# Attention, leaky MLP and bilinear MLP on one core: the second sweep's blocks kept raw, and most accumulating transfers made into adds

## The chip, the core and the metric

One core of one Trainium2 chip runs the whole program. The metric is the device time of one execution, in microseconds. Engines are PE (TensorE), DVE (VectorE), ACT (ScalarE), POOL (GpSimd) and SP, which issues the plain transfers; POOL's queue issues the accumulating ones.

## What is computed

With 4 batches, 8 heads, 576 positions, 64 per head and 32 memory slots:

```
a = softmax(phi, over positions)
k_m, v_m = a^T k, a^T v                      # 32 x 64 for each batch and head
attn = softmax(q k_m^T / 8) v_m              # -> x: 2304 tokens x 512
h = x @ moe_w_in                             # 512 -> 2048
y = max(0.01 h, h) @ moe_w_out               # 2048 -> 512   (first MLP)
out = ((y @ w_a) * (y @ w_b)) @ w_out2       # 512 -> 1536 -> 512   (second MLP)
```

All of it is float32.

## The kernel before

Each matrix product is made as three matmuls of fp32r halves: an operand is split into a rounded copy ("hi", a CAST on ACT or DVE) and the rest ("lo", a subtraction on DVE). Most large products use a seven-product scheme for 2x2 blocks, so sums and differences of blocks (`S1` to `S4` of the weights, `T1` to `T4` of the data) are made on DVE and split too.

**First MLP.** Four chunks `c` of 512 of the 2048 columns, four batches. `v_m` is folded into `w_in` (`vw`, L682), `h` is made from the attention weights (L724, L733), the leaky ReLU gives `bt` (ACT, L700). `y_part` makes the seven products (`ys_x`, `ys_y`, `ys_z`, L873); their results are copied or joined into tiles `ok` and summed into the accumulators `acc` (`acc_of`, one for each batch and half of the columns, 128x1024). From chunk 1 on `y_out` (L892 on) adds a finished `ok` to its `acc` either on DVE or by an accumulating transfer from POOL's queue (L909), as the order table says.

**Second MLP.** Two sweeps `s` (two batches each) over 12 chunks `c` of 128 of the 1536 columns. `ab_unit` makes the seven products `abx`, `aby`, `abz` (L1081) from `yb`, the split blocks of the first MLP's output, and `wo`, the split weights; `left_unit` does the last 64 positions; `p_sums` makes the blocks `pb` of the elementwise product; `o_part` makes the second seven products (`os_x`, `os_y`, `os_z`, L1294) with `w2` (weight sums, `w2_sums`, L1206 on) and `wout2`, and sums into `oacc`, again by DVE or by an accumulating transfer (L1326); `o_unit` (L1159, products `o` L1184) makes what the scheme leaves; `store` writes out.

**What is kept in HBM.** Split weights of the first sweep are stored (`k_wo`, `k_wout`) and loaded back in the second (`w_back`, L1057). `y_blocks` (L942 to L980) makes the blocks of both sweeps as the first MLP ends: for the first sweep seven pairs that stay in SBUF, for the second seven pairs that are stored (14 stores `k_yb`, L965) and loaded back by `y_back` (L982 to L986) as the second sweep begins. `w2_sums` makes the weight sums once and stores the pairs (L1237); `w2_back` (L1197 to L1204) loads them in the second sweep.

**What sets the order.** Every instruction's place in the program is written by hand in the table `ORDER` (one number for each operation, with a suffix `a` for ACT, `v` for DVE, `g` for an accumulating transfer where there is a choice), and every tile's buffer in `PLACES` (37 + 9 buffers of SBUF, `s` and `g`, 6 small ones, 8 PSUM banks `b`). `Program.run` emits in that order; each engine and each queue works in order, and waits arise from data and from buffers that are used again.

Of the kernel before, what the change touches and what calls it, by code (L numbers as in the profile page):

```python
# [8 lines left out]
F32 = mybir.dt.float32  # L9
# [18 lines left out]
NB2 = 512  # L28
# [43 lines left out]
def c_dve(n):  # L72
    return 0.16 + n * 1.03e-3
# [13 lines left out]
9 15 14 17 21 40 12 22 11 8 23 62 43 41 16 7 24 2 44 65 18 46 25 26a 45 67 20 48a 82 84v 13 47 81 1 50a 42 28a 19 6 238 51 52 10 66 53 38 54a 3 29 60 55  # L87
59a 58a 83a 30 31 69 244 56a 57v 70 257 32a 33 250 239 242 71a 34a 35a 72a 39 240 5 4 61 241 91 37a 245 68 80 247 93 36a 92 27 243 79 248 94 258 0 95 246
249 96 252 97 264 261 259 98 99 278 265a 113 63 260 49 64 102 104 262 266a 251 312 263 253 85 254 103 255 313 86a 280 267 105 106 256 87 107 310 269v 270
268v 316 89a 279 117 88a 118 281 108 314 119 317 282 121 109 311 73 272 134 90 136a 78 165 110 74v 327 122 286 294 271 274 273 124v 120 275 315 75 76a 77a  # L90
329 324 283 143 328 321 115 145 144 146 123a 325 472 114 330 116 318 147 322 331a 333a 319 332 133 334 335 148 132 287 135a 295 168 149 338a 336a 170 297
296 288 337 150 348 131 298 154 473 169 339 344 289 151 156 320 155 157 290 184 158 130 159 186a 125 326 152a 160 172 161 153 162 126a 291 299 292v 174a
111a 137 475 476 349a 342 138a 323 478 346 142 300a 185 139 140a 171 127 129a 352 474 276v 277 128a 187a 302 100a 301 484 194 163a 164 195 141a 479 166 196
101 480 359 303 197 198 347 167 183 477 353a 350 487 376 284a 173 175a 343 361 360 379a 351 285 377a 517 380 305 199 200 201 357 205 345a 365 378 518 481
362 181 520 354 182 206 366 207 193 367 340 364 358a 381 202 208 363 355 521 203a 204 501 482 341 356 384a 374a 385 209 372a 375 486 188 176 368a 370a 751
382a 388 373 386 177a 189a 369 210 178 179a 502 190 192a 371 394 519 180a 383 304 389 191a 211 227 212 483 387 390 306a 213 229 503 214a 293 216 396 1316
490 492 391a 395a 1340 397 228 230 215 218 411 522 418 491 504 217 219 220 509 1322 510 231 221 412 222 421a 485 223 400 505 401 224 494 506 405 406 402
407 512 488 403 232 493 233 419a 225a 404a 408 414a 392 393 226 733 398 409 413 234 420 410 422 735 308a 423 415 430 424a 399a 734 431 426a 428 235 432 112
# [12 lines left out]
731a 523a 900 788 732 877 1005 884 782 783 866 807 837a 878 1008 808 524 876g 1006 858 871 791 903a 1367 1369 1007 912 885 859 901a 872 862 838 768a 907
839a 873 1017 863 794 864 850 1011 846 847 852 795 904 851 861 879 769 902 913 886 1374a 1376a 944 1377 867 1014 881 776a 798a 882 868 916 883 1375 840
1012 797 880 921 1416 887a 947a 1390 777 796 799 1009 888 933 908 922a 930 931 889 934 905 917a 1013 1417 906 936 938 925 926 939 1420 1419 937 1418 890a
1389 1020 935 918 1421 800a 891 951 895 932g 920 892 893v 923 801 919 956 924 1023 898a 894 1010 952a 914 915 927 909 945a 820g 899 946 1019 929 957a 960
1018 928 961a 948 1015 967 965 966v 911 910 949 792a 793 896a 897 1392 958 1025 1016 950 1422a 1393 1423 968 959 1021 1022 1026 1424 981 1024 1027 953 940a
954 972 969g 955 942a 941 973 977 962 963 1429 1028 1395 986 982 1398 784v 987 974 976 1029 1081 975 1394 1030a 785 964 970 943 1082a 971 1400 989 983 979
1031 1032a 1033 985 1090 984 990a 1085 980 1401 1091 1076 1077a 991 1083 1058 1084 992 1100 978 1059 1086 1087 998 1399 1402 1089 1088 1095 993a 1074 1099
1101 988g 1060 1396 1397 999a 1408a 1092g 1078 1042 1079 994 1080 1409 1062 1075 1102 995 1061 1003a 996a 1063 1093 1094 1425 1107 997 1108a 1104 1096 1034
1103a 1120 1403 1001a 1050 1000 1004 1002 1125 1043 1045 1410a 1098 1126a 1121a 1127 1128 1129g 1097 1113 1116a 1036 1046 1137 1114a 1117 1404 1106 1115
1132 1052 1141 1035 1105 1405 1130 1407 1406 1037 1414a 1038 1411 1426 1133 1044 1131 1134 1146 1412a 1122 1047 1053 1051 1454 1138 1415 1123 1136 1172  # L120
1413 1124 1147 1179 1142 1436 1173a 1175a 1176 1428 1111a 1135 1054 1039 1427 1184 1040a 1174 1109a 1055 1438 1139 1140 1185 1156 1118 1119 1066 1439 1041
1143 1145 1157 1144 1153 1154 1110 1149 1150 1158 1151 1155 1159a 1188 1048a 1216 1180 1067 1070a 1069 1068 1049 1152 1199 1189a 1071 1164 1217a 1201 1219a
1112 1195 1193 1160 1196 1186 1197 1430 1431 1194a 1218 1187 1202 1198 1716 1437 1208 1200 1170a 1161 1433 1167 1162a 1210 1203 1204g 1177 1440 1441 1207
1163 1171 1165a 1209 1211 1457 1072a 1190 1191 1455 1223 1148g 1192 1456 1220 1073 1178 1166 1442 1448a 1228 1224a 1056a 1432 1449 1057 1434 1181 1458 1205
1229a 1206 1232 1435 1459 1168a 1183 1237 1182 1225 1233a 1239 1464 1064a 1443 1238a 1169 1227 1212a 1230 1253 1226 1554 1231 1221 1444 1234 1222 1214a
1255 1065 1213 1249 1257 1240 1258 1577 1256 1215 1462 1460a 1251 1236 1254 1259 1235 1261 1252 1260g 1244 1242 1461 1246 1277 1467 1250 1262a 1263 1243
1551 1247 1264 1283 1245 1279 1267 1265a 1281 1278a 1268a 1280a 1266 1288 1273a 1521 1270 1271a 1710 1290 1241g 1289a 1269 1284 1291a 1468a 1287 1272 1294
1601 1292 1282 1295a 1274 1520 1470 1719 1293a 1297 1248 1285g 1473 1286 1296 1450a 1298g 1305 1717 1445 1452a 1469 1451 1453 1476 1301 1711 1525 1580 1466
1306 1303 1304 1474a 1299 1477a 1275a 1475 1307g 1606 1302 1276 1526a 1484a 1528 1300 1471a 1481 1552 1314 1485 1516a 1556 1315 1517 1529a 1479a 1312 1446a
1308 1480 1532 1478 1578 1465 1310 1447 1579 1563 1522 1713 1557a 1502 1523 1482a 1507a 1519 1311 1559 1472 1509 1488a 1530 1531a 1558 1553 1492 1565 1581  # L130
# [146 lines left out]
def tile_mem_attention__leaky_mlp__bilinear_mlp(  # L277
# [664 lines left out]
    def y_blocks(s, due):  # L942
# [11 lines left out]
        def pair(name):  # L954
            g, t = at[name]
            hi, lo = ("yb", s, name, 0, 0), ("yb", s, name, 1, 0)
            for k in (hi, lo):
                tile_of(k, "slot", [2, NB2], F32R)
# [441 lines left out]
    for s in range(2):  # L1400
        if s:
            y_back(1)
# [67 lines left out]
```

## Time and profile before

| | us |
|---|---|
| median of 3 runs | 765.59 |
| lowest, highest | 765.35, 765.61 |
| profiled execution, own time | 768.98 |
| its span in the profile | 767.2 |
| PE busy | 750.8 |
| DVE busy | 642.2 |
| ACT busy | 495.8 |
| POOL busy | 29.4 |

The span runs from the first to the last instruction of the profiled execution. A busy share is the mean over stages that differ, so the windows of the section with the rows give it by stretch. An engine's idle piece is put down to what came last before it, by the semaphores that the profile shows.

### The profile page before, as it was taken

The numbers are of one execution on the slowest core, as the hardware profiler recorded it, in microseconds if no ns is written. First come the engines' busy times: TensorE is split into PE (matmuls) and PEld (weight loads), VectorE is DVE, ScalarE is ACT, GpSimd is POOL, SyncE is SP. The second block draws the span as 40 slices with busy tenths as digits, with TensorE's granted clock in tenths as the row PEclk, the third lists the DMA queues.
The fourth block names the chain that finished last, engine by engine and source line by source line (L and its number), as shares of the span: only waits on it lengthen the run. The fifth ranks groups of instructions, "written<-read, shape, count | busy, mean of one in ns | idle before, by whom it ended". The sixth has DMA issues, their size and how long they took to land.

```text
span 767.2 us, 12233 instructions
## 1 busy us (share of the span) xinstructions
PE 750.8 (98%) x4492; PEld 618.0 (81%) x4492; DVE 642.2 (84%) x1040; ACT 495.8 (65%) x975; POOL 29.4 (4%) x39
## 2 busy tenths in 40 slices
PE   8899999999999999989999999999999999999997
PEld 7656778887898878878888888888878888878886
DVE  2888988988799899989988899989999775766776
ACT  4889999778788788856566757686652423333430
POOL 0000000000001000010000000000000000010100
PEclk9999999999999999999999999999999999999999
DMA  8986502535545664578889787797999899797955
GB/s 318 343 328 234 193 1 97 193 97 160 147 133 147 142 194 136 151 226 240 289 303 324 290 256 261 265 303 276 320 378 317 293 310 359 251 248 262 314 114 166
DMA packets 66059, 179.84 MB, mean 234 GB/s; under 512 B 8016, under 2 KB 21584, under 8 KB 66000
## 3 DMA queue, kind: packets, MB, share of 16 engines
q1 hardware_dynamic: 61248, 161.76, 59.7%
q0 software_dynamic: 4752, 17.30, 12.1%
q8 instruction: 35, 0.57, 0.3%
q14 instruction: 24, 0.20, 0.1%
HBM read 109.84 MB, written 51.90 MB: 211 GB/s over the span
## 4 chain that ended last, share of the span: by engine, by line
PE 81%; DMA 6%; ACT 5%; issue 4%; DVE 3%; POOL 0%; SPq 0%; DVEq 0%; POOLq 0%; ACTq 0%
PE abx L1081 14%; PE h L733 12%; PE ys_x L873 9%; PE os_x L1294 7%; PE abz L1081 7%; PE ys_z L873 4%; PE os_z L1294 4%; PE aby L1081 4%; PE o L1184 3%; PE yl L817 2%; PE ys_y L873 2%; PE vw L682 2%; PE a L1126 2%; PE b L1126 2%; PE os_y L1294 2%
## 5 line engine op out<-in xcount | busy, mean ns | idle before, releaser
L1081 PE MATMUL abx<-yb_T,wo 128*128 128x512 f32 x432 | 109.0, 390 | 0.9 <-DMA wo<-k_wo_-1_1_3_2771 0.9
L1081 PEld LDWEIGHTS abx<-yb_T,wo 128*128 128x128 f32 x432 | 80.2, 188 | 17.5 <-issue 1.3
L311 ACT COPY ok<-os_x 128x512 f32<-128x512 f32 x66 | 38.3, 587 | 57.7 <-PE os_x L1294 49.6
L733 PE MATMUL h<-ahi,vwh 128*128 128x320 f32 (+1 forms) x240 | 72.3, 301 | 0.4 <-ACT bt L700 0.4
L733 PE MATMUL h<-alo,vwh 128*128 128x320 f32 (+1 forms) x240 | 71.1, 296 | 0.0
L733 PE MATMUL h<-ahi,vwl 128*128 128x320 f32 (+1 forms) x240 | 71.0, 296 | 0.0
L700 ACT ACTIVATE bt<-h 128x256 f32<-128x256 f32 x120 | 45.6, 389 | 23.1 <-PE h L733 19.7
L733 PEld LDWEIGHTS h<-ahi,vwh 128*128 128x128 f32 x240 | 45.4, 189 | 10.2 <-issue 2.6
L311 ACT COPY pf<-abx 128x512 f32<-128x512 f32 x48 | 27.9, 585 | 36.4 <-PE abx L1081 34.1
L733 PEld LDWEIGHTS h<-alo,vwh 128*128 128x128 f32 x240 | 45.4, 189 | 1.9
L733 PEld LDWEIGHTS h<-ahi,vwl 128*128 128x128 f32 x240 | 45.4, 189 | 0.0
L316 DVE TENSOR_TENSOR sl_T<-bt,sh_T 128x1024 fp32r<-128x1024 f32 x28 | 34.2, 1220 | 8.1 <-ACT sh_T L311 6.0
L1294 PE MATMUL os_x<-pb_T,w 128*128 128x512 f32 x132 | 36.3, 392 | 1.7 <-ACT ok L311 1.6
L1081 PE MATMUL abx<-yb_B,wo 128*128 128x512 f32 x144 | 36.7, 390 | 0.0
L1081 PE MATMUL aby<-yb_B,wo 128*128 128x512 f32 x144 | 36.7, 390 | 0.0
L1081 PE MATMUL abz<-yb_B,wo 128*128 128x512 f32 x144 | 36.6, 391 | 0.1
L1081 PE MATMUL abz<-yb_T,wo 128*128 128x512 f32 x144 | 36.3, 390 | 0.0
L316 DVE TENSOR_TENSOR bt<-bt,bt 128x1024 f32<-128x1024 f32 x28 | 33.8, 1218 | 0.7 <-ACT bt L700 0.4
L311 ACT CAST sh_T<-bt 128x1024 fp32r<-128x1024 f32 x27 | 28.5, 1055 | 6.7 <-DMA k_wout_-1_3932<-wout_-1_3888 3.8
L1081 PEld LDWEIGHTS abz<-yb_B,wo 128*128 128x128 f32 x144 | 26.8, 188 | 6.0 <-DVE u L316 0.5
L1081 PEld LDWEIGHTS abx<-yb_B,wo 128*128 128x128 f32 x144 | 26.8, 188 | 5.9 <-issue 0.4
L1081 PEld LDWEIGHTS abz<-yb_T,wo 128*128 128x128 f32 x144 | 26.9, 188 | 5.7
(318 smaller groups left out, 2011.3 us busy)
## 6 DMA issues: line engine op xcount, KB each, us to landing
k_wo<-wo SPq DMA_DIRECT2D x32, 512.0 KB, 6.5
wo<-k_wo SPq DMA_DIRECT2D x32, 512.0 KB, 5.6
raw_wout<-in_w_out_dram SPq DMA_DIRECT2D x24, 512.0 KB, 4.6
acc<-ok POOLq DMA_DIRECT2D x18, 512.0 KB, 5.1
kv<-in_kv_dram SPq DMA_DIRECT2D x16, 512.0 KB, 9.3
raw_win<-in_w_in_dram SPq DMA_DIRECT2D x16, 512.0 KB, 6.7
oacc<-ok POOLq DMA_DIRECT2D x15, 512.0 KB, 8.0
k_w<-w SPq DMA_DIRECT2D x10, 512.0 KB, 6.0
```

The costliest lines, as they stand in the source:

```text
L311: nc.scalar.copy(dst, src)
L316: nc.vector.tensor_tensor(dst, a, b, op=alu)
L682: nc.tensor.matmul(T[os[i]][k * M:(k + 1) * M, :], vm[half, k, b, :], w, start=True, stop=True)
L700: nc.scalar.activation(dst, src, AF.Prelu, alpha=0.01)
L733: nc.tensor.matmul(T[o], T[w[u]][:, k, fs], T[a[v]][:, k, cols], start=k == 0 and y == 0, stop=k == 1 and y == 2)
L817: nc.tensor.matmul(T[o], T[ws[j]][:, u, w_left(c, 2 * eh + j, i, x)], T[hl[v]][:, f, :], start=f == 0 and y == 0, stop=f == 3 and y == 2)
L873: nc.tensor.matmul(T[o], lhs(T, u, w_left(c, 0, kk, x)), T[hl[v]][:, kk, :], start=i in (1, 2, 5) and kk == 0 and y == 0, stop=kk == 1 and ...
L1081: nc.tensor.matmul(T[o], T[w][:, which, u, k * P:(k + 1) * P], T[ys[v]][:, k, :], start=first and k == 0 and x == 0, stop=k == 1 and x == ...
L1126: nc.tensor.matmul(T[o], T[w][:, k // 2, u, k % 2 * P:(k % 2 + 1) * P], T[ys[v]][:, k, :], start=(k == 0 and x == 0), stop=(k == 3 and x = ...
L1184: nc.tensor.matmul(T[o], T[w][:, u, es], right(T, x, v), start=(x == 0 and k == 0), stop=(x == 1 and k == 2))
L1294: nc.tensor.matmul(T[o], lhs(T, u), T[g][:, v, :], start=i in (1, 2, 5) and k == 0, stop=k == 2, skip_group_check=True)
```

## The change

1. The second sweep's four accumulators `acc(2,·)` and `acc(3,·)` are stored as they are when the first MLP ends (`y_keep`, 4 stores) and loaded raw as the second sweep begins (`y_back`, 4 loads into `acb`). The four differences and the seven splits are made there, the differences in place of the `acb` tiles.
2. `w2_back` and the stores of `w2` are gone; `w2_sums` runs in both sweeps, from `wf`, which is loaded again in the second (5 loads of 512 KB more).
3. Of 33 accumulating transfers 5 are left; the others are adds on DVE.
4. `ORDER` and `PLACES` are new throughout (3065 operations, 3060 before).

```diff
-    def y_blocks(s, due):
+    def y_blocks():
...
-            for k in (hi, lo):
-                if s == 0:
-                    tokens[k] = [k]
-                else:
-                    op("DMA", c_dma(524288), lambda T, k=k: nc.sync.dma_start(kept(k), T[k].bitcast(F32)), r=[k], w=[("kept", k)], tiles=[k], ahead=1e12)
...
+    def y_keep(due):
+        for l in range(2):
+            for j in range(2):
+                g = ("acc", 2 + l, j)
+                op("DMA", c_dma(524288), lambda T, g=g: nc.sync.dma_start(kept(g), T[g]), r=[(g, x) for x in range(2)], w=[("kept", g)], tiles=[g], ahead=1e12, due=due)
+
+    def y_back():
+        at = {}
+        for l, j in ((0, 0), (1, 0), (1, 1), (0, 1)):
+            k, g = ("acb", l, j), ("acc", 2 + l, j)
+            tile_of(k, "slot", [2, NB2])
+            op("DMA", c_dma(524288), lambda T, k=k, g=g: nc.sync.dma_start(T[k], kept(g)), r=[("kept", g)], w=[k], tiles=[k], ahead=40.0)
+            at[f"B{j + 1}{l + 1}"] = k
+        into = {"T1": "B11", "T2": "T1", "T3": "B12", "T4": "B21"}
+        for name, x, y in Y_SUMS:
+            if x:
+                g, a, b_ = at[into[name]], at[x], at[y]
+                op("DVE", c_dve(2 * NB2), lambda T, g=g, a=a, b_=b_: minus(T[g], T[a], T[b_]), r=[a, b_], w=[g], tiles=list(dict.fromkeys((g, a, b_))), ahead=25.0)
+                at[name] = g
+            y_pair(1, name, at[name], [at[name]])
...
-    def w2_back(q):
...
-            if s == 0 and by_seven(1, 2 * q):
-                op(
-                    "DMA", c_dma(524288), lambda T, k=k: nc.sync.dma_start(kept(k).rearrange("p a b -> p (a b)"), flat(T[k])),
...
-                    if s and by_seven(0, c):
-                        w2_back(c // 2)
-                    else:
-                        w2_sums(s, c // 2)
+                    w2_sums(s, c // 2)
```

`y_pair` is the old `pair` without its store: a copy that rounds and a subtraction.

Three places show the order. POOL's queue, all its accumulating transfers after the set-up, here the last ones of before (`acc` are the first MLP's accumulators, `oacc` the second's with the sweep as their first number):

```order
L1326 DMA oacc_0_1_0_4723<-ok2_0_5_6_6726 128x1024
L1326 DMA oacc_1_1_1_7127<-ok2_1_1_7_7244 128x1024
L1326 DMA oacc_1_1_0_7159<-ok2_1_1_6_7198 128x1024
L1326 DMA oacc_1_0_0_7006<-ok2_1_1_1_7191 128x1024
L1326 DMA oacc_1_0_0_7006<-ok2_1_2_1_7422 128x1024
L1326 DMA oacc_1_1_0_7159<-ok2_1_2_6_7469 128x1024
```

and all of the change:

```order
L909 DMA acc_1_0_1235<-ok_3_0_6_3762 128x1024
L1312 DMA oacc_0_0_0_4749<-ok2_0_2_1_5469 128x1024
L1312 DMA oacc_0_1_1_4693<-ok2_0_2_7_5512 128x1024
L1312 DMA oacc_0_1_0_4732<-ok2_0_2_6_5491 128x1024
L1312 DMA oacc_0_0_0_4749<-ok2_0_3_1_5887 128x1024
```

Of 33 rows 5 are left, one on `acc` and four on the first sweep's `oacc`; none is left in the second sweep.

SP's queue where the first sweep begins, before (`k_` is a place in HBM, left of the arrow for a store):

```order
L1057 DMA wo_0_0_1_4244<-k_wo_-1_0_1_1897 128x1024
L965 DMA k_yb_1_B22_1_0_4250<-yb_1_B22_1_0_4168 128x1024
L965 DMA k_yb_1_B21_0_0_4261<-yb_1_B21_0_0_4248 128x1024
L1057 DMA wo_0_1_3_4280<-k_wo_-1_1_3_2771 128x1024
L1033 DMA k_wo_-1_3_0_4324<-wo_-1_3_0_4186 128x1024
L965 DMA k_yb_1_B22_0_0_4337<-yb_1_B22_0_0_4158 128x1024
L965 DMA k_yb_1_B21_1_0_4350<-yb_1_B21_1_0_4287 128x1024
L965 DMA k_yb_1_B11_0_0_4352<-yb_1_B11_0_0_4263 128x1024
```

and with the change:

```order
L1057 DMA wo_0_0_3_4238<-k_wo_-1_0_3_1867 128x1024
L392 DMA raw_wb_7_0_4241<-in_w_b_dram 128x4x128
L1057 DMA wo_0_1_1_4263<-k_wo_-1_1_1_2302 128x1024
L970 DMA k_acc_2_1_4266<-acc_2_1_1690 128x1024
L970 DMA k_acc_3_0_4269<-acc_3_0_1684 128x1024
L392 DMA raw_wa_6_0_4280<-in_w_a_dram 128x4x128
L1057 DMA wo_0_2_1_4305<-k_wo_-1_2_1_3453 128x1024
```

The stores of split blocks are gone from between the loads of `wo`, and two of the four stores of accumulators stand there, each behind nothing but the accumulator itself.

DVE's queue shortly before the second sweep's first product, with the change (`acb` are the raw blocks, `yb_1` the second sweep's split ones, `ok2` the joins of the second MLP):

```order
L316 TENSOR_TENSOR ok2_0_4_6_6283<-os_0_4_0_z_6279,ok2_0_4_6_6283 128x512
L316 TENSOR_TENSOR yb_1_B21_1_6349<-acb_0_1_6313,yb_1_B21_0_6315 128x1024
L316 TENSOR_TENSOR pt_11_6166<-b_11_6222,pt_11_6166 128x256
L316 TENSOR_TENSOR acb_0_0_6007<-acb_1_1_6329,acb_0_0_6007 128x1024
L316 TENSOR_TENSOR acb_1_0_6054<-acb_1_1_6329,acb_1_0_6054 128x1024
L316 TENSOR_TENSOR oacc_0_1_0_4732<-oacc_0_1_0_4732,ok2_0_3_6_6025 128x1024
L316 TENSOR_TENSOR acb_0_1_6313<-acb_0_1_6313,acb_0_0_6007 128x1024
L316 TENSOR_TENSOR oacc_0_0_1_4639<-os_0_4_1_x_6331,oacc_0_0_1_4639 128x512
```

None of the `acb` and `yb_1` rows stood here before; the add on `oacc` is a row of the kind that takes the place of an accumulating transfer.

## Rows read from the trace of the kernel before

**Rows 1.** The page, part 1: busy us, share of the span, instructions.

```profile
PE   750.8 (98%) x4492; PEld 618.0 (81%) x4492; DVE 642.2 (84%) x1040; ACT 495.8 (65%) x975; POOL 29.4 (4%) x39
```

**Rows 2.** Window: us, PE, PEld, DVE, ACT, POOL busy, PEclk, DMA share, GB/s.

```profile
0.00:80.00 80.00, 73.92 (x795) 49.74 (x796) 56.82 (x116) 62.97 (x153) 0.69 (x6) 1.00 0.84 298
```

**Rows 3.** PE's timeline (start, us, what) at five stalls, then its waits.

```profile
339.18 0.50 PE L873 MATMUL ys_x<-sh_T,wsh 128*128 128x512 f32 x1 [1.96 <-ACT ok L311]
...
372.20 1.16 PE L1081 MATMUL abx<-yb_T,wo 128*128 128x512 f32 x4 [0.90 <-DMA wo<-k_wo_-1_1_3_2771]
...
422.85 1.42 PE L1184 MATMUL o<-plf,wout 128*128 128x256 f32 x9 [0.58 <-ACT oaccl L311]
...
511.45 0.98 PE L1184 MATMUL o<-plf,wout 128*128 128x256 f32 x6 [0.63 <-DVE oaccl L316]
...
690.43 0.98 PE L1294 MATMUL os_x<-pb_T,w 128*128 128x512 f32 x3 [1.56 <-ACT ok L311]
...
PE tz L506 <- ACT en L311: 1.8, 1, 1.8
PE h L724 <- DVE at L642: 0.7, 1, 0.7
```

**Rows 4.** Other engines' timeline, and the chain, around those stalls.

```profile
327.34 1.21 DVE L316 TENSOR_TENSOR bt<-bt,bt 128x1024 f32<-128x1024 f32 x1
327.72 1.75 POOL L909 DMA_DIRECT2D acc<-ok  x2 [17.12 <-DVE ok L316]
328.48 0.68 DVE L316 TENSOR_TENSOR wout_-1_3888<-cv_wout,wout_-1_3888 128x512 fp32r<-128x512 f32 x1
329.22 0.32 SPq L1033 DMA_DIRECT2D k_wout_-1_3932<-wout_-1_3888  x1
337.60 1.04 ACT L311 CAST sh_T<-bt 128x1024 fp32r<-128x1024 f32 x1 [3.79 <-DMA k_wout_-1_3932<-wout_-1_3888]
...
353.11 10.22 DMA acc<-ok
...
360.04 7.29 SPq L965 DMA_DIRECT2D k_yb_B<-yb_B  x2
363.35 0.62 ACT L311 CAST wo_-1_3_0_4186<-cv_wab 128x512 fp32r<-128x512 f32 x1 [5.16 <-DMA acc<-ok]
...
409.62 8.70 DMA raw_wa<-in_w_a_dram
...
507.51 0.62 ACT L311 CAST wout<-cv_wout 128x512 fp32r<-128x512 f32 x1 [2.74 <-DMA oacc<-ok]
...
678.33 10.37 DMA oacc<-ok
```

**Rows 5.** Accumulating transfers: issues by kind, KB each, median us to landing.

```profile
acc<-ok POOLq DMA_DIRECT2D x18, 512.0 KB, 5.1
oacc<-ok POOLq DMA_DIRECT2D x15, 512.0 KB, 8.0
```

**Rows 6.** DVE's groups by line and form: busy us, mean ns of one, idle before.

```profile
L316 DVE TENSOR_TENSOR oacc<-oacc,ok 128x1024 f32<-128x1024 f32 x12 | 14.6, 1216 | 0.0
L316 DVE TENSOR_TENSOR w<-w2s,w 128x512 fp32r<-128x512 f32 x12 | 8.2, 685 | 1.3 <-ACT w L311 1.3
L316 DVE TENSOR_TENSOR w2s<-wf 128x256 f32<-128x256 f32 x12 | 4.8, 416 | 1.7 <-DMA wf<-k_wf 1.7
L447 DVE TENSOR_REDUCE nmx<-phi 128x2 f32<-128x1152 f32 x3 | 4.0, 1345 | 1.6 <-DMA phi<-in_phiT_dram 1.6
```

**Rows 7.** Windows between marks that both orders have, columns as above.

```profile
520.20:597.70 77.50, 76.98 (x385) 64.23 (x384) 72.34 (x130) 42.25 (x78) 0.00 (x0) 1.00 0.88 320
597.70:683.30 85.60, 85.60 (x382) 70.96 (x382) 60.24 (x95) 30.17 (x55) 3.44 (x4) 1.00 0.88 292
683.30:767.20 83.90, 78.29 (x343) 62.90 (x341) 57.31 (x88) 26.62 (x46) 6.07 (x7) 1.00 0.74 219
```

**Rows 8.** A window of 20 us with DVE nearly full, same columns.

```profile
460.00:480.00 20.00, 20.00 (x115) 17.52 (x114) 19.67 (x40) 15.66 (x31) 0.00 (x0) 1.00 0.72 266
```

More of the change, by code (lines that the diff above doesn't have):

```diff
@@ L940, in kept @@
         return places[k]
-    def y_blocks(s, due):
-        acc = lambda l, j: ("acc", 2 * s + l, j)
-        made = lambda l, j: [((acc(l, j)), x) for x in range(2)]
-        yt = {n: ("yt", s, n) for n in ("T1", "T2", "T3", "T4")}
-        at = {f"B{j + 1}{l + 1}": (acc(l, j), made(l, j)) for j in range(2) for l in range(2)}
-        at.update({n: (k, [k]) for n, k in yt.items()})
-        def minus_of(name, x, y):
-            tile_of(yt[name], "slot", [2, NB2])
-            (a, ta), (b_, tb) = at[x], at[y]
-            op("DVE", c_dve(2 * NB2), lambda T: minus(T[yt[name]], T[a], T[b_]), r=[*ta, *tb], w=[yt[name]], tiles=[yt[name], a, b_], ahead=1e12, due=due)
-        def pair(name):
-            g, t = at[name]
-            hi, lo = ("yb", s, name, 0, 0), ("yb", s, name, 1, 0)
-            for k in (hi, lo):
-                tile_of(k, "slot", [2, NB2], F32R)
-            op(copy_by(2 * NB2), 0, lambda T, e: copy(e, T[hi], T[g]), r=t, w=[hi], tiles=[hi, g], ahead=1e12, due=due)
-            op("DVE", c_dve(2 * NB2), lambda T: minus(T[lo], T[g], T[hi].bitcast(F32)), r=[*t, hi], w=[lo], tiles=[hi, lo, g], ahead=1e12, due=due)
-            for k in (hi, lo):
-                if s == 0:
-                    tokens[k] = [k]
-                else:
-                    op("DMA", c_dma(524288), lambda T, k=k: nc.sync.dma_start(kept(k), T[k].bitcast(F32)), r=[k], w=[("kept", k)], tiles=[k], ahead=1e12)
-                    back = (*k[:4], 1)
-                    tile_of(back, "slot", [2, NB2], F32R)
-                    tokens[back] = [back]
-        pair("B11")
-        minus_of("T1", "B12", "B11")
-        pair("T1")
-        minus_of("T2", "B22", "T1")
-        pair("T2")
-        minus_of("T3", "B22", "B12")
-        pair("T3")
-        pair("B21")
-        minus_of("T4", "B21", "T2")
-        pair("T4")
-        pair("B22")
@@ L982, in y_back, with y_pair @@
-    def y_back(s):
-        for name in YB:
-            for i in range(2):
-                k, back = ("yb", s, name, i, 0), ("yb", s, name, i, 1)
-                op("DMA", c_dma(524288), lambda T, k=k, back=back: nc.sync.dma_start(T[back].bitcast(F32), kept(k)), r=[("kept", k)], w=[back], tiles=[back], ahead=25.0)
+    def y_pair(s, name, g, t, due=None):
+        k = [("yb", s, name, v) for v in range(2)]
+        for x in k:
+            tile_of(x, "slot", [2, NB2], F32R)
+            tokens[x] = [x]
+        ahead = 25.0 if s else 1e12
+        op(copy_by(2 * NB2), 0, lambda T, e: copy(e, T[k[0]], T[g]), r=t, w=[k[0]], tiles=[k[0], g], ahead=ahead, due=due)
+        op("DVE", c_dve(2 * NB2), lambda T: minus(T[k[1]], T[g], T[k[0]].bitcast(F32)), r=[*t, k[0]], w=[k[1]], tiles=[*k[::-1], g], ahead=ahead, due=due)
@@ new lines, in tile_mem_attention__leaky_mlp__bilinear_mlp @@
+    Y_SUMS = (("B11", None, None), ("T1", "B12", "B11"), ("T2", "B22", "T1"), ("T3", "B22", "B12"), ("B21", None, None), ("T4", "B21", "T2"), ("B22", None, None))
+    def y_blocks():
+        acc = lambda l, j: ("acc", l, j)
+        at = {f"B{j + 1}{l + 1}": (acc(l, j), [(acc(l, j), x) for x in range(2)]) for j in range(2) for l in range(2)}
+        for name, x, y in Y_SUMS:
+            if x:
+                g = ("yt", name)
+                tile_of(g, "slot", [2, NB2])
+                (a, ta), (b_, tb) = at[x], at[y]
+                op("DVE", c_dve(2 * NB2), lambda T, g=g, a=a, b_=b_: minus(T[g], T[a], T[b_]), r=[*ta, *tb], w=[g], tiles=[g, a, b_], ahead=1e12)
+                at[name] = (g, [g])
+            y_pair(0, name, *at[name])
@@ new lines, in y_keep @@
+    def y_keep(due):
[11 more added lines that the diff above has]
+        into = {"T1": "B11", "T2": "T1", "T3": "B12", "T4": "B21"}
+        for name, x, y in Y_SUMS:
+            if x:
+                g, a, b_ = at[into[name]], at[x], at[y]
+                op("DVE", c_dve(2 * NB2), lambda T, g=g, a=a, b_=b_: minus(T[g], T[a], T[b_]), r=[a, b_], w=[g], tiles=list(dict.fromkeys((g, a, b_))), ahead=25.0)
+                at[name] = g
+            y_pair(1, name, at[name], [at[name]])
@@ L1075, in product @@
             i, which = PLACE[left]
-            w, ys = ("wo", s, c, i), [("yb", s, right, v, s) for v in range(2)]
+            w, ys = ("wo", s, c, i), [("yb", s, right, v) for v in range(2)]
             def prod(T):
@@ L1195, in o_unit @@
             store(s, l, e, acc, i, (ka, cut[0]) if cut else ka, cut)
-    def w2_back(q):
-        for i in range(2):
-            k, there = ("w2", 1, q, i), ("w2", 0, q, i)
-            tile_of(k, "slot", [2, 2, 256], F32R)
-            op(
-                "DMA", c_dma(524288), lambda T, k=k, there=there: nc.sync.dma_start(flat(T[k]), kept(there).rearrange("p a b -> p (a b)")),
-                r=[("kept", there)], w=[k], tiles=[k], ahead=40.0,
-            )
     def w2_sums(s, q):
@@ L1234, in w2_sums @@
             )
-            if s == 0 and by_seven(1, 2 * q):
-                op(
-                    "DMA", c_dma(524288), lambda T, k=k: nc.sync.dma_start(kept(k).rearrange("p a b -> p (a b)"), flat(T[k])),
-                    r=[k], w=[("kept", k)], tiles=[k], ahead=1e12,
-                )
     def p_sums(s, q, odd):
@@ L1395, in tile_mem_attention__leaky_mlp__bilinear_mlp @@
     pr.due = None
-    y_blocks(0, None)
+    y_blocks()
     y_left_blocks()
-    y_blocks(1, (step + 1, 0))
+    y_keep((step + 1, 0))
     queue = []
@@ L1401, in tile_mem_attention__leaky_mlp__bilinear_mlp @@
         if s:
-            y_back(1)
+            y_back()
         for c in range(NC2):
```

257 lines of the change are left out of this document (128 added, 129 removed).

## The prediction

> **What bounds the kernel now.** I read the busy table first. TensorE (PE) is busy for 750.8 of 767.2 us with 4492 matmuls [rows 1]; the change leaves their number and shapes as they are, so only PE's 16.4 us of idle time can be won, and anything that adds idle time is lost at once. Next I read the windows: 6.1 us of the idle time lie in the first 80 us (80.00 less 73.92, [rows 2]) and 5.6 from 683.3 on (83.90 less 78.29, [rows 7]), the rest in small pieces; PE's granted clock reads 1.00 in each of these rows, which here is the 2.4 GHz level, so clock plays no part. PE's own timeline and list of waits [rows 3] name what came last before each idle piece, and most names are ACT or DVE. So I followed each back through the chain and the other engines' timelines [rows 4], and there five stalls turn out to be made by transfers:
> - At 339.18 PE waits 1.96 us for ACT. ACT itself stood 3.79 us until the store of `wout` had read its buffer. That store was issued at 329.22, just behind two accumulating transfers issued at 327.72, and had still not let go of its buffer 8 us later.
> - At 372.20 PE waits 0.90 us for a load of `wo`. SP (the queue of plain transfers) was held for 7.29 us from 360.04 on by two stores of `yb_B` ahead of it; those hung on ACT, which stood 5.16 us for an accumulating transfer that took 10.22 us.
> - At 422.85, 0.58 us: behind a load of `raw_wa` that took 8.70 us.
> - At 511.45, 0.63 us: ACT had stood 2.74 us for an accumulating transfer.
> - At 690.43, 1.56 us: ACT's `ok`, and before it ACT's `pb_B`, came behind an accumulating transfer of 10.37 us that ended at 688.70.
>
> Together 5.6 us. In three of the five an accumulating transfer of `ok` is the cause itself; in the others the queues are crowded. The list of transfers shows why those are bad to wait for: a median of 5.1 (`acc`) and 8.0 us (`oacc`) from issue to landing [rows 5].
>
> **The change, part by part.**
> *Transfers.* 10 stores and 10 loads of split blocks go (14 of each become 4), 10 stores and 10 loads of split weight sums become 5 loads, and 28 of 33 accumulating transfers go: 63 transfers of 0.524 MB, 33 MB. The four first-MLP blocks that are stored now are the accumulators themselves, so no split stands ahead of their stores, and the two stores that held SP at 360.04 don't exist. ACT's waits at 363, 507 and 689 have no accumulating transfer left to wait for: after the change only one `acc` and four `oacc` transfers remain, all before the second sweep. I take all five stalls as gone, −5.6 us; the bounds are −5.6 and 0 (each replaced by a wait of its own length).
>
> A page speaks against the cause. The Trainium skill, DMA: Bandwidth & Descriptors, section Anatomy of one DMA — SWDGE (gpsimd) path, has a transfer from this queue last about 2.0 us and its bytes at 436 GB/s, which for 524288 bytes would be an estimate of 3.2 us. This case's rows don't agree: their medians are 5.1 and 8.0 us, and 10.22 and 10.37 on the chain. By that rule nothing of the 5.6 us would come back, and the time would be that of rival 1.
>
> *DVE's added work.* 28 adds of 128x1024 at 1.216 us (17 on `acc`, 11 on `oacc`) are 34.0 us [rows 6]. The five sets of weight sums made again cost 5 × (4 × 0.416 + 2 × 0.685) = 15.2 us. The subtractions and splits of the `yb` blocks are as many as before, only later. DVE thus goes from 642 us [rows 1] to about 690 of 760. Where it lies decides. I went through DVE's rows in both orders between marks that both have (the first `pf<-abx` of a chunk) and summed them by the means of [rows 6] and their like. Up to 520.2 us the sums differ by 7.8 us in all (2.8 of small copies before 109.7, 6 in 109.7 to 347.7, 1 less after that, since 7 splits leave). DVE's free time there is 67.8 us: 767.2 less 642.2 for the whole span [rows 1], less 5.2, 25.4 and 26.6 in the three stretches behind 520.2 [rows 7]. So I count nothing. From 520.2 (chunk 8 of the first sweep) to 597.7 (first chunk of the second) it is 7.1 more: 4 subtractions and 6 splits arrive, older weight work leaves. From 597.7 to 683.3 it is 27.2 more: 19 rows of weight sums, 8 splits of them, 3 adds, and joins that were done later before. After 683.3 it is 11.6 more, in 26.6 us of free time.
> So the stretch 520.2 to 683.3 has to take 34.3 us. From that I subtract the overlap of neighbours: the rows at 327.34 and 328.48 start 1.14 us apart where the first lasts 1.21 [rows 4], 0.07 us for each of 50 added rows, 3.5 us. That leaves 30.8. The stretch has 5.16 + 25.36 = 30.5 us free on DVE [rows 7]. How far can gaps be filled? In the 20 us from 460 on DVE is busy 19.67 and PE all 20.00 [rows 8]; so a nearly full DVE doesn't stop PE by itself, but 1.65% stays open, 2.7 us of 163.1. DVE's cost is 0.3 + 2.7 = **+3.0 us**. The lower bound is 0 (work runs on past 683.3, where time is free). For the upper one, if only two thirds of the gaps can be filled, because DVE works in order and a gap is a wait for a product, it is 30.8 − 20.3 = +10.5. I take the low value since the row at a full DVE is the nearest one.
>
> *Prologue.* The phi reduction of batch 1 is put first on DVE, and between the score transposes and the first `at` DVE now does one clamp and one join of weights, not two each, some 1.1 us less. The first `h` waits 0.7 us for exactly this `at` [rows 3]. I take −1.0. At best the 1.8 us wait of `tz` goes with it (−2.5); at worst the reduction ahead of everything (1.345 us, [rows 6]) delays the first scores as a whole (+1.4).
>
> *The raw blocks' latency.* SP has the first two loads of `acb` among the stores of chunks 9 and 10, well ahead of the second sweep's first product. 0; at worst one more stall like that at 372, +0.9 [rows 3].
>
> *The tail.* PE's last products stand in the same order. Three `oacc` adds stand among DVE's last joins, one before, beside the last nine groups of `o` products. 0; at worst the two more, +2.4 [rows 6].
>
> Sum: −5.6 + 3.0 − 1.0 = −3.6 us. The profiled execution took 768.98 (span 767.2) and would take 765.4; it lies 3.4 above the median of the runs, 765.59, so against that median the forecast is **762.0 us**.
>
> **Rivals.**
> 1. *Accumulating transfers were not what held PE.* If a transfer that is short on its own only looked late because ACT or SP reached its consumer late, the 5.6 us stay in another form: −1.0 + 3.0 = +2.0, **767.6 us**. For it: two of five stalls name no accumulate. Against it: 10.22 and 10.37 us measured on the very chain. The rule of the Trainium skill quoted above would make this case.
> 2. *Waits only change places.* The adds that were DMA's stand in DVE's line, and `ok` buffers come free later; gains and losses are equal when 79% of DVE's gaps get filled (30.8 − 0.79 × 30.5 = 6.7, against 5.6 + 1.0). About **765.6 us**, 1.5 to both sides.
> 3. *DVE becomes the bound between the sweeps (slower).* Between 520 and 683 DVE has to do 30.8 us more in gaps of 30.5. With two thirds of the gaps filled the cost is 10.5: −6.6 + 10.5 = +3.9, **769.5 us**. It decides below 79%. For it: 72.34 of 77.5 us are already in use at 520 to 598, and the gaps that are left there are in-order waits. Against it: the full windows, and free time behind 683.3 for work that isn't urgent.
> 4. *The relief is larger.* With 33 of 180 MB gone, the transfers that remain land earlier, DVE's overload runs on into the free tail at no cost, and the prologue gives its best: −5.6 − 2.5 = −8.1, **757.5 us**.
>
> **How the numbers follow.** Forecast 0.46, larger relief 0.18, waits only move 0.13, rival 1 0.05, DVE as the bound 0.18. Two per mille, 1.5 us, is what a measurement of this kernel can tell from no change; faster means below 764.1, slower above 767.1. Forecast and larger relief are faster; rival 1 and rival 3 are slower; rival 2, at no change, reaches a little to either side: faster 0.65, same 0.13, slower 0.22. The range goes from 756.0 (rival 4 less its last 1.5 us) to 769.5 (rival 3 at two thirds); beyond lie half of rival 3 and a little of rival 4.
>
> **What the profile would show.** If right: POOL's transfers are 5, ACT's list of waits has no entry for `acc<-ok` or `oacc<-ok`, PE has no idle pieces near 339, 372, 511 and 690, and some 33 MB less is moved. DVE is busy near 690 us, with over 95% between 520 and 683 and PE above 99% there. The first `h` no longer waits 0.7 us for `at`. It is wrong if PE's waits name DVE (`pb`, `yb_T`, `w`) with more than some 3 us in 520 to 683 (rival 3), if ACT waits for plain transfers as long as it did for accumulating ones (rival 1), or if the first 80 us lose more than 6.1 us.

## The result, and the profile after

The changed kernel takes **758.29 us** (median of 4 runs, 757.93 to 759.62) against 765.60 for the kernel before beside it: a ratio of 0.9908, 95% interval 0.9891 to 0.9925. The gain is 7.3 us, twice the forecast 3.6, and the time lies in the range of 756.0 to 769.5, next to rival 4 (757.5). The profiled execution took 758.21 us, span 756.4.

The page's busy table and its line of transfers (as [rows 1]):

```profile
PE 745.9 (99%) x4492; PEld 616.8 (82%) x4492; DVE 687.1 (91%) x1117; ACT 496.3 (66%) x966; POOL 5.1 (1%) x11
...
DMA packets 56987, 146.80 MB, mean 194 GB/s; under 512 B 7009, under 2 KB 20577, under 8 KB 56929
```

DVE is busy 45 us longer, PE's idle time went from 16.4 to 10.5 us and its busy time from 750.8 to 745.9, and 33.0 MB less is moved. The windows show where PE's idle time went. Columns as in [rows 2]: stretch, us, busy time of PE, PEld, DVE, ACT, POOL, granted clock, share of the DMA engines, GB/s.

```profile
0.00:80.00 80.00, 74.69 (x806) 49.81 (x807) 61.20 (x132) 64.81 (x150) 0.70 (x6) 1.00 0.82 306
320.00:360.00 40.00, 40.00 (x208) 34.49 (x207) 39.27 (x45) 26.17 (x40) 1.00 (x1) 1.00 0.46 154
520.00:600.00 80.00, 80.00 (x398) 67.65 (x397) 78.54 (x131) 45.55 (x80) 0.86 (x1) 1.00 0.73 255
600.00:680.00 80.00, 80.00 (x354) 66.23 (x353) 69.21 (x117) 30.25 (x55) 0.00 (x0) 1.00 0.70 240
```

Between 320 and 360, where the store of `wout` and the accumulating transfers had cost nearly 2 us, PE is full, though DVE is busy 39.27 of 40. From 520 to 680 PE has no gap at all; DVE is at 98% in the first half of that and at 87% in the second. In the first 80 us PE is idle for 5.3 us in place of 6.1. Rows of PE's list of waits (in total, times, longest), as [rows 3]:

```profile
PE b L1126 <- ACT pt L311: 0.8, 1, 0.8
PE h L733 <- ACT bt L700: 0.8, 1, 0.8
PE os_y L1280 <- DVE oacc L316: 0.8, 1, 0.8
PE sc L598 <- ACT vwf L311: 0.8, 1, 0.8
PE tz L506 <- ACT en L311: 0.6, 1, 0.6
```

None of the five stalls of [rows 3] is left, and neither is the wait of `h` for `at`; `tz` waits 0.6 in place of 1.8. Behind the first 80 us one stall is new: `b` at 387.28 waits 0.8 us for ACT. On the chain there stand a store of `wo` that took 8.63 us and then another of 4.83: split weights, made ahead, are written out to be read again.

```profile
371.77 8.63 DMA k_wo_-1_3_1_4409<-wo_-1_3_1_4260
...
380.88 4.83 DMA k_wo_-1_3_2_4430<-wo_-1_3_2_4303
...
386.97 0.27 ACT pt L311
387.24 0.04 issue
387.28 2.77 PE b L1126 x21
```

### The profile page after: what moved, and what is told of

It reads as the page before. It is cut to its first block, busy times and chain, and to the rows that moved or that the text cites. A ratio compares the mean times of both kernels' runs of the same rounds, so it can differ in the third digit from the quotient of the medians.

```text
span 756.4 us, 12134 instructions
## 1 busy us (share of the span) xinstructions
PE 745.9 (99%) x4492; PEld 616.8 (82%) x4492; DVE 687.1 (91%) x1117; ACT 496.3 (66%) x966; POOL 5.1 (1%) x11
## 4 chain that ended last, share of the span: by engine, by line
PE 91%; DMA 4%; DVE 3%; ACT 1%; issue 0%; SPq 0%; ACTq 0%; DVEq 0%
PE abx L1081 16%; PE h L733 13%; PE ys_x L873 10%; PE os_x L1280 8%; PE abz L1081 8%; PE ys_z L873 5%; PE aby L1081 4%; PE os_z L1280 4%; PE o L1184 4%; PE yl L817 3%; PE ys_y L873 3%; PE vw L682 2%; PE b L1126 2%; PE a L1126 2%; PE os_y L1280 2%; PE y L786 1%
## 5 line engine op out<-in xcount | busy, mean ns | idle before, releaser
L1081 PEld LDWEIGHTS abx<-yb_T,wo 128*128 128x128 f32 x432 | 80.5, 188 | 16.4
L733 PE MATMUL h<-ahi,vwh 128*128 128x256 f32 (+1 forms) x240 | 72.7, 303 | 0.8 <-ACT bt L700 0.8
L733 PE MATMUL h<-ahi,vwl 128*128 128x256 f32 (+1 forms) x240 | 71.0, 296 | 0.0
L733 PE MATMUL h<-alo,vwh 128*128 128x256 f32 (+1 forms) x240 | 71.0, 296 | 0.0
L311 ACT COPY u<-abx 128x512 f32<-128x512 f32 x24 | 14.0, 585 | 31.4 <-PE abx L1081 31.3
L1081 PEld LDWEIGHTS aby<-yb_B,wo 128*128 128x128 f32 x144 | 26.8, 188 | 5.5
```

Of the source, the lines that this page charges most:

```text
L311: nc.scalar.copy(dst, src)
L733: nc.tensor.matmul(T[o], T[w[u]][:, k, fs], T[a[v]][:, k, cols], start=k == 0 and y == 0, stop=k == 1 and y == 2)
L1081: nc.tensor.matmul(T[o], T[w][:, which, u, k * P:(k + 1) * P], T[ys[v]][:, k, :], start=first and k == 0 and x == 0, stop=k == 1 and x == ...
```

## The experiments

Three theories were to be told apart. **Transfers:** the accumulating transfers themselves held PE up, through ACT and DVE, and DVE has room for the adds. **Order:** the new order made the gain, whatever carries the adds. **Crowding:** fewer bytes did it.

### 1. The old kernel with adds only

```diff
-                o.fn(tiles, engine[word[-1]])
+                e = engine[word[-1]]
+                if "DMA" in o.costs:
+                    e = "DVE"
+                o.fn(tiles, e)
```

> The kernel before, with all 33 accumulating transfers made as adds on DVE, at the places in the order where the transfers stood; nothing else is changed. If ACT's and PE's waits for accumulating transfers were the cause (the forecast's first term), the stalls at 372, 511 and 690 go, and the one at 339 too if the store there was late because of the two accumulates ahead of it: 5.1 us less at most, so 760.5 to 763.5 us, with DVE at about 680 us busy. If the gain of the change came from the new order alone, this gives nothing, and 33 adds (40 us) in DVE's old queue make it 766 to 772. If the gain came from fewer bytes in general, only 17 of the 33 MB go: 762 to 764, and the waits for plain transfers at 339 and 422 stay.

Measured: 780.39 us against 765.22, ratio 1.0192 (1.0167 to 1.0218); slower than all three cases, so each of them missed the cost of the adds in this order. PE's waits for transfers are gone and waits for DVE stand in their place: `ys_x` for `sl_T` 1.9 us in four pieces, `os_y` for `oacc` 1.9, `abx` for `yb_B` 1.5, `o` for `oacc` 1.2. One of them in DVE's and PE's timeline (start, us, what, and what it waited for):

```profile
269.17 1.22 DVE L319 TENSOR_TENSOR acc<-acc,ok 128x1024 f32<-128x1024 f32 x1
270.31 1.22 DVE L319 TENSOR_TENSOR sl_T<-bt,sh_T 128x1024 fp32r<-128x1024 f32 x1
...
271.58 0.50 PE L876 MATMUL ys_x<-sl_T,wsh 128*128 128x512 f32 x1 [0.73 <-DVE sl_T L319]
```

An add stands just ahead of a split that PE needs, and PE waits until both are done. In the old order the adds cost 15 us net.

### 2. The new kernel with 33 accumulating transfers

```diff
-                o.fn(tiles, engine[word[-1]])
+                e = engine[word[-1]]
+                if "DMA" in o.costs:
+                    e = "DMA" if o.tiles[0] in OLD else "DVE"
+                o.fn(tiles, e)
```

`OLD` are the 33 `ok` tiles that the kernel before sent by transfer.

> The changed kernel, with the same 33 adds as in the kernel before made by accumulating transfers again (28 more than now, 2 of its own 4 on oacc back to adds where the old kernel had adds). If accumulating transfers were the cause, stalls of ACT and PE for them come back, and the time rises by 3 to 6 us to 761 to 764.5, although DVE has 34 us less to do. If the new order made the gain, it stays at 758.3, or gets a little faster (756 to 758) because DVE is relieved.

Measured: 775.39 us, ratio to the kernel before 1.0128 (1.0100 to 1.0157), that is 17 us over the changed kernel, although DVE had 31 us less to do (656.2 busy). The direction is that of the first theory, the size far over it: the new order counts on an add being done 1.2 us after its turn, and a transfer is done some 5 us after. In the chain and the timelines:

```profile
171.11 4.93 DMA acc<-ok
...
176.12 1.04 ACT L314 CAST sh_B<-bt 128x1024 fp32r<-128x1024 f32 x1 [3.29 <-DMA acc<-ok]
...
177.50 0.49 PE L736 MATMUL h<-ahi,vwh 128*128 128x320 f32 x1 [1.93 <-ACT bt L703]
```

So both exchanges lose: order and assignment are made for each other, and experiments 1 and 2 don't tell what a transfer costs by itself.

### 3. and 11. Exchanged prologues

Experiment 3 gives the changed kernel the first 300 operations in the old order, experiment 11 the old kernel the first 290 in the new order; buffers are those of the donor where they fit. The first line of `ORDER` in the two:

```diff
 ORDER = """
-62 65 16 4 40 43 14 44 6 12 13 3 1 17 2 8 67 66 238 41 7 47 46 69 50a ...
+9 15 14 17 21 40 12 22 11 8 23 62 43 41 16 7 24 2 44 65 18 46 25 26a 45 ...
```

and the reverse in the other.

> The changed kernel, with its first 300 operations (of 3065) in the order, on the engines and, where it fits, in the buffers of the kernel before. The traces show the first y product at 45.2 us before and at 42.7 us after, 2.5 us earlier. If that lead is kept to the end, this kernel is 2 to 2.7 us slower than the change, 760.3 to 761.0. If PE's later waits swallow it (DVE and ACT are the bound of the first 80 us and only catch up later), it is within 0.7 us of 758.3.

> The kernel before with the first 290 operations in the order, on the engines and, where it fits, in the buffers of the changed kernel; the rest of its order as it was. If the prologue's gain is a part by itself, 2 to 4 us faster than the kernel before (the traces differ by 2.1 us of PE time in the first 80 us; the reverse exchange cost 6 us): 761.5 to 763.5. If a prologue only pays with the order that follows it, within 1 us of the kernel before or slower.

Measured: 764.24 us (762.20 to 767.11) for experiment 3, 6 us over the change; 768.26 (764.63 to 771.40) for experiment 11, ratio 1.0018 (1.0002 to 1.0035), 2 us over the kernel before. Experiment 3 is slower than either case that was expected; experiment 11 is the second case, a prologue that pays only with the order that follows it. Both kernels have stalls that neither original has: in experiment 3 `h` waits 1.0 us for `tl` and `vw` 0.5 for `vwl`, and the wait of `b` near 390 grows from 0.8 to 2.2 us; in experiment 11 an `h` waits 2.1 us for `bt` at the seam, 64.76 us. A prologue can't be moved by itself, so these runs don't give its part.

### 4. The old kernel again

> The kernel before once more, to see which of its stalls belong to every execution. Its profiled execution took 768.98, 3.4 us over the median. If stalls made by transfers vary from one execution to the next, this look shows other sizes or places for them (about 765.6, PE idle some 13 us in place of 16.4), and the difference to the change of 7.3 is what the medians show. If they are the same each time, PE's idle time is 16.4 us again.

Measured: 764.17 us in one execution, span 762.4, PE busy for 749.1 and so idle for 13.3, as the first case has it. Three of the five stalls are there, in other sizes; those at 422 and 511 are not:

```profile
339.04 0.50 PE L873 MATMUL ys_x<-sh_T,wsh 128*128 128x512 f32 x1 [1.77 <-ACT ok L311]
...
371.57 1.61 PE L1081 MATMUL abx<-yb_T,wo 128*128 128x512 f32 x6 [0.39 <-DMA wo<-k_wo_-1_1_3_2771]
...
685.55 0.97 PE L1294 MATMUL os_x<-pb_T,w 128*128 128x512 f32 x3 [0.47 <-ACT ok L311]
```

Stalls that transfers make vary from one execution to the next, 2.6 us here and 5.6 in the first profile, and with them the time.

### 5. and 6. More work on DVE between the sweeps

```diff
             else:
                 o.fn(tiles)
+                if o.eng == "DVE" and o.tiles and o.tiles[0][:2] in (("yb", 1), ("w2", 1)):
+                    for _ in range(1):
+                        o.fn(tiles)
```

(`range(2)` in experiment 6).

> The changed kernel, with every lo-split of the second sweep's yb blocks (7 of 1.22 us) and weight sums (10 of 0.685 us) made twice on DVE, one right after the other: 15.4 us more DVE work, all between about 540 and 700 us; the result is the same. After the change DVE has about 1 us free in 540 to 600, 11 in 600 to 680 and 8.5 behind that, while PE has no idle time there. If DVE's gaps can be filled (as the forecast's DVE term has it), most of it is swallowed: 0 to 4 us slower, 758.3 to 762.5. If DVE is the bound there already, or only two thirds of its gaps can be filled, it is 8 us or more slower, 766 to 774.

> As the last, with these splits made three times: 30.7 us more DVE work than in the changed kernel, against some 20 us of free time from 540 us on. If gaps can be filled, about 30.7 less 20 and what the run before showed: 10 to 14 us slower, 768 to 773. If every us on DVE counts in full, 30 us slower, 788.

Measured: 769.08 us with 15.4 us of added work, 785.47 with 30.7: 10.8 and 27.2 us over the change. The first lies in the range of DVE as the bound (766 to 774), the second between its two cases, nearer to that in which all of it counts. The first 15.4 us cost 0.70 us for each us, the next 15.3 cost 16.4, all of it. PE now waits for DVE in many small pieces:

```profile
PE o L1187 <- DVE oaccl L319: 2.2, 3, 1.0
...
PE aby L1084 <- DVE pf L319: 1.0, 1, 1.0
...
PE os_z L1283 <- DVE oacc L319: 0.7, 1, 0.7
PE os_x L1283 <- DVE w L319: 0.7, 1, 0.7
PE os_z L1283 <- DVE ok L319: 0.7, 2, 0.3
```

So the change brought DVE near its limit between the sweeps, with some 5 us to spare (15.4 less 10.8), and not over it. A split that is made twice is also ready later itself, and PE's waits name such a split, `w` or `yb_B`, with 1.2 us in all; the two effects weren't parted further. Rival 3 has the right place, and what lies beyond the limit costs time as it said; only the limit isn't reached.

### 7. Plain transfers in place of the accumulating ones

```diff
+                if "DMA" in o.costs and e == "DVE" and o.tiles[0] in OLD:
+                    self.beside(o.tiles[0])
...
+    def beside(k):
+        there = hbm.tile([P, 2, S], F32, name="beside_" + "_".join(map(str, k)))
+        nc.sync.dma_start(there, qT[len(used) % 4, len(used) // 4 % 2])
+        used.append(k)
```

> The changed kernel with its adds on DVE, but at each of 30 places where the kernel before had an accumulating transfer, a plain transfer from SP's queue from HBM to another place in HBM (576 KB, 17.7 MB in all) that no instruction waits for and that holds no buffer. It tells crowded queues from buffers that are held. If the number of bytes and of transfers was what made the stalls, 2 to 6 us slower, 760 to 764. If what counts is that an accumulating transfer holds its ok and acc tiles, it stays within 1 us of 758.3.

Measured: 760.91 us, 2.6 us over the change, which by the time alone lies in the range expected of crowding. The ratio to the kernel before beside it is 0.9923 (0.9906 to 0.9939) where the change has 0.9908 (0.9891 to 0.9925), 1.1 us apart, and the intervals overlap. So 30 more transfers with 17.7 MB cost between nothing and some 3 us, and PE's list of waits shows no stall of 0.5 us or more behind a transfer after the first 80 us. Crowding isn't the main cause; a small part of it is not excluded. These transfers go from HBM to HBM in SP's queue, so what accumulating ones do in POOL's queue is not copied here.

### 8. Adds as late as they can be

Each add is moved back to 8 places ahead of the first operation that needs its result or its buffer; for instance

```diff
-660g 537a 1382 672 538 597 646 647 648 655 1381 675a 657 637 656 667 ...
+537a 1382 672 538 597 646 647 648 655 1381 675a 657 637 656 667 660v ...
```

> The kernel before with all 33 transfers made as adds on DVE, as in the first experiment (780.4), but each add moved back in the order to 8 places ahead of the first operation that needs its result or its buffer (0 to 88 places later, 18 on the mean). If the first experiment lost because adds stood ahead of urgent splits and joins in DVE's queue, much of the 15 us comes back: 766 to 772. If it lost because DVE simply had too much to do, it stays at 778 to 782.

Measured: 778.03 us (776.04 to 779.99), 2 us less than experiment 1, in the range of the second case. But it isn't the amount: DVE is busy 676.7 us here and 687.1 in the changed kernel, which is 20 us faster. Getting the adds out of the way of the next few operations doesn't bring the loss back; in the new order the whole of DVE's queue is laid out around them.

### 9. and 10. Transfers and adds left out

Nothing takes their place, so the sums in `acc` and `oacc` lack these parts, and the cost of each way of adding is seen by itself.

```diff
-                o.fn(tiles, engine[word[-1]])
+                if not ("DMA" in o.costs and word[-1] == "g"):
+                    o.fn(tiles, engine[word[-1]])
```

in the kernel before (experiment 9), and in the changed kernel the same for the adds on DVE of the `ok` tiles in `OLD` (experiment 10).

> The kernel before without its 33 accumulating transfers: they are left out, and nothing takes their place, so the sums in acc and oacc lack those parts. It shows what those transfers cost by themselves, with no add on DVE. If they make the stalls at 339, 372 and 690 (1.9, 0.5 and 0.6 us in the second look at the kernel before, 2.0, 0.9 and 1.6 in the first, and at 511 in the first), PE has none of them, and the time falls by 3 to 5 us to 760.5 to 762.5. If other waits stand behind those stalls, it falls by less than 1.5 us.

> The changed kernel without 30 of its 40 adds of ok tiles on DVE (those that the kernel before made by transfers): left out, so sums lack those parts, and DVE has 36.5 us less to do. If DVE's added adds cost the changed kernel nothing, because they stand where DVE has room, it stays within 1 us of 758.3. If part of the possible gain is still held back by a full DVE, it is 2 to 4 us faster, 754.5 to 756.5, with fewer of PE's waits at 387 and in the last 20 us.

Measured: experiment 9 takes 759.57 us against 766.03, ratio 0.9913 (0.9892 to 0.9934): without its accumulating transfers the old kernel, in its old order, is 6.5 us faster (5.1 to 8.3 by the interval), a little more than expected. PE's stalls at 339, 372, 511 and 690 are gone; the one at 422 is there, behind the same kind of load as in [rows 4]:

```profile
416.25 0.67 ACT L403 ACTIVATE cv_wab<-raw_wa 128x512 f32<-128x512 f32 x1 [2.39 <-DMA raw_wa<-in_w_a_dram]
...
420.68 1.54 PE L1185 MATMUL o<-plf,wout 128*128 128x256 f32 x10 [0.99 <-ACT oaccl L312]
```

Experiment 10 takes 758.57 us, ratio 0.9895 (0.9878 to 0.9913), where the change has 0.9908 (0.9891 to 0.9925): the changed kernel isn't measurably faster without 30 of its adds. DVE has 33 us less to do, and PE is as full as with them:

```profile
80.00:320.00 240.00, 240.00 (x1562) 203.04 (x1561) 210.95 (x303) 197.02 (x406) 0.00 (x0) 1.00 0.34 113
520.00:600.00 80.00, 80.00 (x398) 67.64 (x397) 78.83 (x132) 45.66 (x81) 0.86 (x1) 1.00 0.74 255
586.13:681.32 95.19, 95.19 (x422) 78.76 (x421) 80.32 (x139) 38.14 (x70) 0.00 (x0) 1.00 0.65 220
```

These two settle the main question. The transfers cost 6.5 us where they stood; the adds that took their place cost nothing that these runs can tell from noise. Some 21 of the 33 us lie ahead of 520 us, and the weight sums that are made again stay in experiment 10.

### 12. The last five transfers as adds

The edit of experiment 1, made in the changed kernel.

> The changed kernel with its last 5 accumulating transfers made as adds on DVE too, at their places: 6.1 us more on DVE, five of them at 350 to 560 us where DVE is busy over 95%. The run with splits made twice showed 0.7 us for each us added behind 540; by that 3 to 5 us slower, 761 to 763.5. If one of the five transfers holds something up now, it could be the same or faster, 757 to 759.

Measured: 762.98 us, ratio to the kernel before 0.9961 (0.9946 to 0.9977), 4.7 us over the change. It falls into the range expected. Four of the five stand ahead of 520 us, near 324 and 491 to 499, and one at 545, where DVE is nearly full. The wait of `b` near 390 grows to 2.0 us. No kernel of these beats the change.

## Why the prediction came out as it did

**What bounds the kernel: right in the main.** PE's matmuls are the same 4492. But idle time was not all that could be won: of the 10.8 us between the two profiled spans 5.9 are idle time and 4.9 busy time of PE, and between the second look at the kernel before (experiment 4) and the change it is 2.8 and 3.2. Why the same matmuls are busy for less time stays open.

**Transfers, −5.6 us: right in cause, and the size agrees.** Experiment 9 puts them at −6.5 (−5.1 to −8.3). The stalls at 339, 372 and 690 stand in both profiles of the kernel before and go when nothing but the transfers goes, the one at 339 by way of a late store. The one at 511 goes too, but experiment 4 lacks it as well, so its cause is not shown. The one at 422, which the forecast gave to crowded queues, is in experiment 9 and not in experiment 4; it comes and goes without them. That the sum of five idle pieces came near has luck in it: the forecast took them from an execution 3.4 us over the median, and the second look has 2.6 us for the same stalls.

**DVE's added work, +3.0 us: the term that was wrong.** The traces put it at 0. The amount was right: busy time went up by 45 us, the forecast said about 48. The step that failed is the account of the stretch between the sweeps, which set 30.8 us of work against 30.5 us of gaps between two marks taken from the kernel before. In the changed kernel these marks stand elsewhere:

```profile
507.19:586.13 78.94, 78.94 (x399) 67.01 (x398) 78.05 (x134) 48.37 (x86) 0.86 (x1) 1.00 0.84 302
586.13:681.32 95.19, 95.19 (x421) 78.79 (x420) 83.79 (x142) 38.49 (x71) 0.00 (x0) 1.00 0.64 219
```

DVE's busy time between them is 161.8 us, where the forecast had 132.6 + 30.8 = 163.4. But the stretch lasts 174.1 us, not 163.1: the first mark is passed 13 us earlier than before [rows 7], the last one only 2, and 820 matmuls lie between them in place of 767. The new order moved PE's products too, so 11 us more were free than was counted. PE is busy in all of both parts, the first with DVE at 98.9% (78.05 of 78.94), so the 1.65% kept open for gaps cost no idle time either. Experiment 10 fits this but tests little of it: of its 33 us of adds only 3.5 lie between these marks (83.79 against 80.32 in the second part, nothing in the first). That the estimate was near the edge is shown by experiments 5 and 6: of 15.4 us more some 5 are swallowed, and the rest costs more than the gain.

**Prologue, −1.0 us: right in direction, too small.** The first 680 products are the same in both orders by their tiles. The windows that hold just these, for the kernel before, its second look, the change, and experiments 9 and 10:

```profile
0.00:74.01 74.01, 67.93 (x680) 45.15 (x680) 51.16 (x105) 57.09 (x138) 0.69 (x6) 1.00 0.88 317
0.00:74.10 74.10, 67.50 (x680) 44.70 (x680) 51.18 (x105) 57.16 (x138) 0.70 (x6) 1.00 0.87 316
0.00:71.57 71.57, 66.26 (x680) 43.25 (x680) 52.94 (x115) 56.77 (x129) 0.70 (x6) 1.00 0.88 328
0.00:75.48 75.48, 68.29 (x680) 45.40 (x680) 51.19 (x105) 57.03 (x138) 0.70 (x6) 0.98 0.87 310
0.00:71.75 71.75, 66.98 (x680) 44.30 (x680) 52.92 (x115) 56.69 (x129) 0.69 (x6) 1.00 0.89 328
```

The change is there 2.4 to 2.5 us earlier than the kernel before, of which only 0.8 to 1.3 are idle time. That is the forecast's best case (−2.5), with the wait of `tz` gone from 1.8 to 0.6 and that of `h` for `at` gone. The exchange of prologues (experiments 3 and 11) could not show it as a part by itself.

**Behind the prologue.** From these windows' ends to the end of the span it is 693.2 us in the first profile of the kernel before and 688.3 in the second, but 684.7 to 684.8 in the change and in experiments 9 and 10 alike. So the transfers cost 3.6 to 8.5 us there, by the execution, and the old order without them is as fast as the changed kernel. The blocks kept raw, the weight sums made again and the 18 MB that they save show no gain of their own; each figure is of one execution.

**Raw blocks and tail, 0: right.** `yb_B` waited 0.9 us on ACT for a load of `acb` and PE waited for none of it; the wait of `os_y` for `oacc` in the tail is 0.8 as before.

**The sum.** −6.5 by experiment 9, 0 for DVE, −2.4 for the prologue by the traces, against it 0.8 for the new stall of `b`: −8.1, and −7.3 was measured (−5.7 to −8.3 by the interval). The forecast's −3.6 fell short by its DVE term, +3.0, and by 1.4 us of prologue; the range held because its low end allowed for both. The prologue's 2.4 us is in the traces alone: the medians of experiments 9 and 10, which have the old and the new prologue, are only 1.0 us apart.

**The signs.** Five transfers in POOL's queue, PE's five stalls gone, 33 MB less and PE above 99% between 520 and 683 came as said, and ACT's list of waits names no `acc<-ok` or `oacc<-ok`. DVE over 95% in that stretch did not: it is 98% up to 600 and 87% from there to 680.

**The rivals.** Rival 1 falls by experiment 9. The Trainium skill (DMA: Bandwidth & Descriptors, section Anatomy of one DMA — SWDGE (gpsimd) path) leads to an estimate of 3.2 us for such a transfer; here the medians are 5.1 and 8.0 us before [rows 5], and 4.93 on the chain of experiment 2. Rival 2 is what the old order does (experiments 1 and 8: more than the gain goes into waits for DVE), but not the new one. Rival 3 describes the next step beyond the change (experiments 5, 6). Rival 4 had the right size. Its prologue at the best case is in the traces. DVE's work cost nothing, though not because it ran on into the free tail: there was no overload. That the transfers that remain land earlier is so for some (loads of `wo`, median 5.6 before and 4.8 after) and not for others (`raw_wout`, 4.6 and 5.1), and experiment 7 leaves between nothing and some 3 us for it.

## What to carry to other kernels

Price a transfer that adds in place by what it holds: source and target stay taken for 5 to 10 us, and the engine that wants either of them next passes the wait on to the bound engine. Moving such work onto an engine that is 84% busy can cost nothing or 15 us, by where it stands in that engine's queue; count free time between marks of the new order, not of the old one, and test by leaving the work out on both sides (experiments 9 and 10), since exchanges between two orders measure mostly the misfit. To see what one stretch gained, take the time at which the same products are done, and not the idle time alone.

## What had not been expected of the hardware

After some of the longer stalls PE's granted clock fell for a few us. In experiment 12 PE waited 2.0 us up to 389.95, in experiment 3 2.2 us up to 393.02; the kernel before waited 1.96 us up to 339.18 and kept its clock. In experiment 9 `tz` waited 2.49 us up to 11.11, and the clock of its window of 75.48 us above is 0.98; in experiment 4 it waited 2.34 us and the clock stayed at 1.00. Windows of 3 or 4 us of the three, in that order (the number behind the five engines is the clock):

```profile
388.00:392.00 4.00, 2.04 (x12) 2.05 (x13) 2.33 (x5) 3.54 (x8) 0.00 (x0) 0.83 1.02 410
392.00:396.00 4.00, 4.00 (x22) 3.74 (x22) 3.79 (x8) 2.70 (x5) 0.00 (x0) 0.74 0.51 186
```

```profile
392.00:396.00 4.00, 2.98 (x19) 2.98 (x20) 3.23 (x6) 4.00 (x9) 0.00 (x0) 0.81 0.94 374
396.00:400.00 4.00, 4.00 (x23) 3.70 (x23) 3.83 (x9) 2.33 (x5) 0.00 (x0) 0.77 0.42 137
```

```profile
337.00:340.00 3.00, 1.04 (x5) 0.69 (x5) 1.33 (x2) 2.40 (x4) 0.00 (x0) 1.00 1.02 397
340.00:344.00 4.00, 4.00 (x19) 3.02 (x17) 3.45 (x5) 3.21 (x6) 0.83 (x1) 1.00 0.82 315
```

A reading of 0.74 over 4 us is a mean of the full level (2.4 GHz) and the lower one (1.2 GHz). So a stall of this length can cost more than its idle time; the forecast had counted on a clock of 1.00 throughout.
